# Five output stores issued in two column halves, so that the last store uses SyncE's last completion semaphore

**Chip and metric.** One core of one Trainium2 chip. The metric is the device time of one execution in microseconds (us), lower is better.

## The reference

A gated linear attention over 768 steps feeds a mixture of four dense experts; every expert is computed for every token.

```python
def _attn_ref(q, k, v, f_logit):            # (4, 8, 768, 48) each
    f = 1.0 / (1.0 + np.exp(-f_logit))
    for t in range(S):
        state = f[:, :, t, :, None] * state + einsum('bhd,bhe->bhde', k[:, :, t], v[:, :, t])
        y[:, :, t] = einsum('bhd,bhde->bhe', q[:, :, t], state)

def _moe_ref(x, domain_probs, w1, w2):      # x: (3072, 384); w1: (4, 384, 1024); w2: (4, 1024, 384)
    p = domain_probs / (domain_probs.sum(-1, keepdims=True) + 1e-09)
    for e in range(4):
        out += p[:, e:e + 1] * (np.maximum(x @ w1[e], 0.0) @ w2[e])
```

## The kernel before

The kernel works through six chunks of 128 time steps (`c`), each with four batches (`nt` or `b`). It keeps a list of steps, orders them with a small plan of its own and then issues them in that order. The output tile of (c, nt) is 128 x 384 in float32, 192 KB, and is stored by SyncE. Only the very last tile, (5,3), is already finished and stored in two column halves.

```python
    def store(c, nt, cols):
        r0 = nt * S + c * T
        nc.sync.dma_start(out=out[r0:r0 + T, cols], in_=tl("o", c, nt)[:, cols])
    ...
    def add_o(c, e, nt, half):
        by_cols = (c, e, nt) == (C - 1, E - 1, B - 1)
        part = half if by_cols else 0
        cols = slice(half * Din // 2, (half + 1) * Din // 2) if by_cols else slice(0, Din)
        ...
            if e == E - 1:
                P.add(f"store {c}.{nt}.{part}", {"DMA": 0.6}, lambda _: store(c, nt, cols), p - 25, deps=[ev], frees=[("o", c, nt)])
    ...
    with _tile.TileContext(nc) as tc:
        tile_hgrn2_outer__then__branch_train_merge_kernel(tc, *args)
```

Some words used below. SyncE is the engine that here issues transfers and waits for them. A semaphore is a counter by which one piece of work tells another that it is done; a wait is *satisfied* if its counter is already there when it is asked. A transfer has *landed* when it has reported that its last bytes are written. An *eviction* copies a result of the matmuls out of their accumulator memory. A *drain* is the instruction by which an engine lets its own work finish, and a *barrier* makes all engines wait for each other.

No line of the kernel says which semaphore a transfer reports to. The framework gives SyncE's transfers eight completion semaphores in turn, HW0 to HW7, and at the end of the program it makes SyncE wait for all of them in that order:

```
the end of SyncE's program, kernel before (one line is one instruction)
transfer: store (5,3), second half     -> reports to HW2
wait  DMASW7, DMASW6
wait  HW0, DMASW5
wait  HW1, DMASW4
wait  HW2, DMASW3        <- the last store
wait  HW3, DMASW2
wait  HW4, DMASW1
wait  HW5, DMASW0
wait  HW6, DVE
wait  HW7, Activation
drain (waits for Pool), first barrier of the engines, second barrier
```

## Time and profile before

| | kernel before |
|---|---|
| time, median of the first 3 runs | 298.62 us (298.36 to 298.94) |
| span of the profile | 296.6 us |
| TensorE busy | 97% |
| last eviction on VectorE ends | 293.68 us |
| last store issued, landed | 293.709, 295.348 us |
| SyncE's wait for it ends, its drain starts | 295.365, 295.733 us |

The last two rows come from the trace's own records of SyncE, which have nanoseconds; the views round to 0.1 us. "Landed" is the moment of the last of the 16 increments of the transfer's semaphore.

### The profile page before, as it was taken

Reading aid. Unit: us, or ns where it says so; the run is one execution under the profiler, and the core shown is the slowest. Engines: PE = TensorE matmul, PEld = TensorE weight load, DVE = VectorE, ACT = ScalarE, POOL = GpSimd, SP = SyncE. Lnnn points to the kernel's source line nnn. Section 1 sums busy time; section 2 is a strip of 40 time slices with the busy share of each in tenths; the row PEclk is TensorE's granted clock in tenths of the full one; section 3 lists DMA queues with packets and bytes.
Section 4 is the critical chain, followed back from the end, with each engine's and each line's share of the span. In section 5 each row is a group of like instructions: output and inputs, shape, how many; then the busy total and the mean of one; then the engine's idle time right before and its main releaser. Section 6 shows DMA issues by size and latency. Waiting matters only on the chain.

```text
span 296.6 us, 5591 instructions
## 1 busy us (share of the span) xinstructions
PE 289.0 (97%) x2172; PEld 170.0 (57%) x2172; DVE 126.1 (43%) x250; ACT 174.3 (59%) x317; POOL 106.1 (36%) x180
## 2 busy tenths in 40 slices
PE   6899999999999999999999999999999999999995
PEld 2476555567777775555555555555555555555553
DVE  6786012785763673045375235243523222101223
ACT  5656656666684667777477575554475544465440
POOL 5786401138767448144449372243220000000000
PEclk9999999999999999999999999999999999999999
DMA  7999999998979999998979932102432100200002
GB/s 157 200 169 206 207 192 210 189 210 167 201 152 166 191 171 185 209 187 164 198 133 218 179 60 35 27 0 67 122 61 30 27 2 27 80 2 0 0 2 106
DMA packets 136462, 36.43 MB, mean 123 GB/s; under 512 B 126812, under 2 KB 135644, under 8 KB 136436
## 3 DMA queue, kind: packets, MB, share of 16 engines
q1 hardware_dynamic: 125188, 29.35, 52.0%
q0 software_dynamic: 11248, 6.72, 16.4%
q8 instruction: 17, 0.28, 0.4%
q14 instruction: 9, 0.07, 0.1%
HBM read 31.51 MB, written 4.72 MB: 122 GB/s over the span
## 4 chain that ended last, share of the span: by engine, by line
PE 78%; DMA 14%; POOL 3%; SPq 2%; issue 1%; ACT 1%; DVE 0%; POOLq 0%
PE ps_m L389 37%; PE ps_m L374 35%; DMA w_sb<-in_moe_w_dram 10%; DMA k<-in_k_dram 4%; SPq L237 2%; POOL w_sb L246 2%; PE ps_t L325 2%; PE ps_t L340 1%; PE ps_t L336 1%; PE ps_t L273 1%; POOL vb L233 1%; PE ps_t L346 1%; ACT e L293 1%; DVE o L396 0%; ACT xT L226 0%
## 5 line engine op out<-in xcount | busy, mean ns | idle before, releaser
L385 ACT ACTIVATE h<-ps_m 128x512 bf16<-128x512 f32 (+2 forms) x188 | 102.4, 548 | 91.9 <-PE ps_m L374 88.9
L374 PE MATMUL ps_m<-xT,w_sb 128*128 128x512 bf16 (+3 forms) x708 | 152.8, 339 | 0.6 <-ACT xT L226 0.6
L389 PE MATMUL ps_m<-w_sb,h 128*128 128x384 bf16 (+1 forms) x776 | 152.6, 324 | 0.1
L389 PEld LDWEIGHTS <-h 128*128 128x128 bf16 x776 | 75.0, 98 | 59.0 <-DMA w_sb<-in_moe_w_dram 0.3
L396 DVE SCALAR_TENSOR_TENSOR o<-ps_m,pn,o 128x384 f32<-128x384 f32 (+1 forms) x73 | 44.5, 612 | 117.3 <-PE ps_m L389 111.1
L374 PEld LDWEIGHTS <-w_sb 128*128 128x128 bf16 x708 | 65.3, 98 | 43.5 <-issue 0.7
L301 POOL TENSOR_TENSOR qk<-q,e 128x384 bf16<-128x384 f32 x18 | 21.4, 1195 | 36.5 <-ACT e L293 34.3
L360 POOL TENSOR_TENSOR Sf<-Sf,egs 48x192 f32<-48x192 f32 x40 | 20.2, 504 | 36.5 <-DVE Sf L353 34.4
L329 DVE TENSOR_TENSOR AT<-ps_t,mask 128x512 bf16<-128x512 f32 x48 | 30.2, 683 | 5.1 <-PE ps_t L325 5.1
L383 DVE TENSOR_SCALAR h<-ps_m 128x256 bf16<-128x256 f32 (+2 forms) x40 | 19.3, 499 | 26.5 <-PE ps_m L374 13.1
L293 ACT ACTIVATE e<-ps_t 128x384 f32<-128x384 f32 x48 | 26.7, 668 | 5.0 <-PE ps_t L273 3.5
L301 POOL TENSOR_TENSOR qk<-k,e 128x384 bf16<-128x384 f32 x20 | 20.2, 1013 | 8.7 <-ACT e L293 5.5
L353 DVE TENSOR_TENSOR Sf<-Sf,ps_t 48x192 f32<-48x192 f32 x40 | 14.0, 350 | 10.3 <-PE ps_t L346 9.4
L246 POOL DMA_DIRECT2D w_sb<-in_moe_w_dram x11 | 8.8, 807 | 18.5 <-DMA k<-in_k_dram 17.2
L361 POOL CAST sb<-Sf 48x192 bf16<-48x192 f32 x40 | 13.6, 340 | 2.6
L398 ACT ACTIVATE o<-ps_m,pn 128x384 f32<-128x384 f32 x22 | 12.8, 582 | 2.5 <-PE ps_m L389 1.5
L644 PE MATMUL ps_m<-busy 128*128 128x512 bf16 x34 | 10.9, 423 | 1.5 <-DVE busy L144 1.5
L265 ACT ACTIVATE ex<-f 128x768 f32<-128x768 f32 (+1 forms) x14 | 10.4, 746 | 1.8 <-DMA f<-in_f_logit_dram 1.8
L298 POOL DMA_DIRECT2D egs<-e x16 | 9.0, 563 | 6.9 <-ACT e L293 6.9
L340 PE MATMUL ps_t<-vb,AT 128*128 128x48 bf16 x192 | 11.4, 184 | 0.0
L269 ACT ACTIVATE gp<-ex 128x768 bf16<-128x768 f32 (+1 forms) x14 | 10.5, 751 | 0.3
L340 PEld LDWEIGHTS <-AT 128*128 128x128 bf16 x192 | 9.9, 97 | 1.1
(54 smaller groups left out, 120.6 us busy)
## 6 DMA issues: line engine op xcount, KB each, us to landing
out_dram<-o SPq DMA_DIRECT2D x23, 192.0 KB, 2.0
w_sb<-in_moe_w_dram POOLq DMA_DIRECT2D x5, 768.0 KB, 18.0
k<-in_k_dram SPq DMA_DIRECT2D x10, 384.0 KB, 5.6
q<-in_q_dram SPq DMA_DIRECT2D x10, 384.0 KB, 5.5
v<-in_v_dram SPq DMA_DIRECT2D x10, 384.0 KB, 5.7
f<-in_f_logit_dram SPq DMA_DIRECT2D x9, 384.0 KB, 4.6
w_sb<-in_moe_w_dram POOLq DMA_DIRECT2D x6, 384.0 KB, 9.0
f<-in_f_logit_dram SPq DMA_DIRECT2D x6, 192.0 KB, 3.8
```

What stands on the lines that cost most here:

```text
L246: ins["w", i] = nc.gpsimd.dma_start(out=w[:, e, ks, cols], in_=r[e][:, ks, cols])
L293: nc.scalar.activation(out=o, in_=i, func=AF.Exp, scale=1.0 if j else -1.0)
L301: engines[eng].tensor_tensor(out=tl("qk", c, b)[:, j, :, 0:D].rearrange("t (i r) d -> t i r d", r=2), in0=tl("qk"[j], c, b // 2)[:, hh(b), ...
L329: nc.vector.tensor_tensor(out=tl("AT", c, b)[:, r].rearrange("s i t -> s (i t)"), in0=tl("A", c, b, r).rearrange("s i t -> s (i t)"), in1= ...
L340: nc.tensor.matmul(out=y[:, h * D:(h + 1) * D], lhsT=AT[:, r, i, :], rhs=vb[:, h, :], start=(c == 0), stop=True, skip_group_check=True)
L353: nc.vector.tensor_tensor(out=Sf[rows, b], in0=Sf[rows, b], in1=KV[rows, :, r, :], op=ALU.add)
L360: nc.gpsimd.tensor_tensor(out=Sf[rows, b], in0=Sf[rows, b], in1=eg, op=ALU.mult)
L374: nc.tensor.matmul(out=hp(c, e, fc, n0, n1, nf)[:, f], lhsT=w1_sb[:, e, kk, (fc + f) * 128:(fc + f + 1) * 128], rhs=tl("xT", c)[:, kk, n0: ...
L383: nc.vector.tensor_relu(out=dst, in_=src)
L385: nc.scalar.activation(out=dst, in_=src, func=AF.Relu)
L389: nc.tensor.matmul(out=tl("op", c, e, nt, part)[:, cols], lhsT=tl("h", c, e, half_of(c, nt * T))[:, fc, nt * T:(nt + 1) * T], rhs=w2_sb[:, ...
L396: nc.vector.scalar_tensor_tensor(out=o, in0=op, scalar=pe, in1=o, op0=ALU.mult, op1=ALU.add)
```

## The change

The intent is to move the last store from HW2 to HW7, so that no wait for an already complete semaphore stands between its landing and the end. Five more transfers in front of it do that, since the semaphores go in turn. They are got by cutting five earlier stores in two.

```diff
+    halved = [(C - 3, B - 1)] + [(C - 2, nt) for nt in range(B)]
+
     def store(c, nt, cols):
         r0 = nt * S + c * T
-        nc.sync.dma_start(out=out[r0:r0 + T, cols], in_=tl("o", c, nt)[:, cols])
+        parts = [slice(i * Din // 2, (i + 1) * Din // 2) for i in range(2)] if (c, nt) in halved else [cols]
+        for p in parts:
+            nc.sync.dma_start(out=out[r0:r0 + T, p], in_=tl("o", c, nt)[:, p])
```

## The prediction

> **What bounds the kernel now.** I read the head of the page first, then the chain of work that ended last, then the last microseconds of that chain, and only then SyncE (SP), which the page hardly mentions because all of it is sequencer work and none of it counts as busy.
>
> ```profile
> span 296.6 us, 5591 instructions
> PE 289.0 (97%) x2172; PEld 170.0 (57%) x2172; DVE 126.1 (43%) x250; ACT 174.3 (59%) x317; POOL 106.1 (36%) x180
> ...
> PE 78%; DMA 14%; POOL 3%; SPq 2%; issue 1%; ACT 1%; DVE 0%; POOLq 0%
> ```
>
> TensorE is busy for 97% of the span and is 78% of the chain. The chain for 286 to 297 us shows how it ends: 44 output matmuls of line 389, then one 0.42 us eviction on VectorE that ends at 293.68 us. Columns are start, length, what.
>
> ```profile
> 287.35 5.88 PE ps_m L389 x44
> 293.24 0.03 issue
> 293.26 0.42 DVE o L396
> ```
>
> From 293.68 to 296.6 no compute runs: these 2.9 us are the last store and the end of the program. The chain view stops short of them, so I asked SyncE's own waits from 293.9 us on (total us, times, longest), and which instructions the two lines concerned issue there (durations in ns, first and last start in us).
>
> ```profile
> SPq L674 <- DMA out_dram<-o: 1.1, 3, 0.6
> SPq L674 <- PEq L674: 0.7, 2, 0.5
> ```
>
> ```profile
> L404 SPq DMA_DIRECT2D out_dram<-o x5: 332/333/350, 290.0 to 293.7; - x5
> ...
> DMA to landing us min/median/max: 1.6/1.8/1.9
> ```
>
> ```profile
> L674 SPq EVENT_SEMAPHORE x6: 28/28/28, 295.4 to 295.7; - x6
> ```
>
> The last line is asked for the window 295.3 to 295.72 us alone. The last store is issued at 293.71 us and lands 1.64 us later, at 295.348. Then SyncE runs six wait instructions. The first is the one that waits for this store. The other five wait for semaphores that are long complete, and still take up 295.4 to 295.7. The trace's records, finer than the view's tenths, have their starts at 295.365, 295.427, 295.486, 295.547, 295.607 and 295.668, and the drain that follows at 295.733. So one satisfied wait costs 0.0606 us from start to start (0.303 us over five), of which the profile reports 0.028 as execution.
>
> Why five are left is in the built program: at the end SyncE waits, in this fixed order, for the DMA completion semaphores HW0, HW1, ... HW7 (each wait shared with one other semaphore), after one wait for two of GpSimd's DMA semaphores. DMAs of SyncE take HW0 to HW7 in turn. In the kernel before the last store is on HW2, so HW3 to HW7 are asked after it.
>
> **What the Trainium skill says.** "Perfetto Trace Analysis", section "Sequencer-only Instruction (DRAIN, etc)": the profiler reports execution alone, and neither the wait before it nor the readiness for the next instruction. The trace agrees: 28 ns is reported of a 60 ns step, so the step and not the duration is the cost. "Advanced Engine Details and Errata", section "Network/Comms": reading a semaphore's value from a sequencer takes 50 to 100 ns on trn2. The 60 ns step here lies in it, although each instruction names two semaphores. "DMA: Bandwidth & Descriptors", section "Anatomy of one DMA — SWDGE (gpsimd) path": most of a DMA's fixed cost of about 2 us is the receipt that its last byte has landed. Here the last 96 KB store, on the hardware path, needed 1.64 us to land and the 192 KB stores about 1.9: halving the bytes saves little, and nothing in the change shortens the last store.
>
> **The change part by part.** Five stores of 192 KB, tiles (3,3) and (4,0) to (4,3), become two of 96 KB each. The order of the built programs shows what else moves.
>
> Added on SyncE: five DMA issues. One issue is 0.33 us, with its semaphore wait and the gap some 0.38 (the store at 213.012 is followed by the next transfer at 213.447, 0.435 later, including a two-semaphore wait). The sum is 5 x 0.38 = 1.9 us of SyncE time. Beside what does it lie? SyncE's timeline around the first one:
>
> ```profile
> 207.66 5.68 SPq L404 DMA_DIRECT2D out_dram<-o  x3
> 213.45 1.24 SPq L314 DMA_TRANSPOSE QK<-qk  x1
> 216.59 4.32 SPq L318 DMA_TRANSPOSE xT<-yb  x2
> ```
>
> The second half of (3,3) pushes the transpose at 213.45 to about 213.83. It then ends its issue at 215.07 instead of 214.69. The next transfer, at 216.59, waits for its input, so 1.5 us of slack take up the 0.38 and nothing later moves. The delayed transpose lands at about 216.9 instead of 216.5, and its matmuls (line 325) run at 226.8. The four stores of (4,x) are issued at 249.8, 252.4, 255.0 and 257.5, 2.6 us apart, with nothing behind them until 289.99. On the path: 0.
>
> Added on the DMA rings: no bytes. 128 packets of 1,536 bytes become 256 of 768 per store, 640 more of 136,462, in stretches where the DMA share is 0.36 (200 to 215 us) and 0.06 (250 to 288 us). On the path: 0.
>
> Added waits elsewhere: three wait instructions on ScalarE and three on VectorE, because a reused output buffer now waits for two halves. The kernel's two reused buffers of tiles (4,0) and (4,1) are first written at 264.7 and 267.3, against second halves landing at about 252 and 254.5: 12 us of slack, so none blocks. On ScalarE the wait is taken while the 0.60 us eviction before it runs. VectorE idles there for 2 us at a time for TensorE. On TensorE the count of instructions and their order are the same, with other semaphore numbers. On the path: 0.
>
> Moved: ten halves where there were five stores shift all later SyncE DMAs by five places in the turn, so the last store goes from HW2 to HW7. A DMA also waits for the one eight places earlier on its semaphore. With the halves these eight places span less time, but the closest pair I find is about 15 us apart in issue (the transpose of 221.00 behind that of 206.28, which landed at 209.34), and the final five stores wait for stores of 250 to 258 us. No new wait.
>
> At the end: HW0 to HW4 are waited for before 294.4, HW5 (store landed 294.411) and HW6 (294.691) pass as HW0 and HW1 did, HW7 passes at 295.365, and the drain follows one step later at 295.43 instead of 295.733. What comes after, the two barriers between the engines, starts when SyncE arrives last (VectorE, the next to last, arrived at 293.745), and keeps its length: 296.6 - 295.73 = 0.87 us. The sum is -5 x 0.0606 = -0.303 us: a span of 296.3, and 298.62 - 0.30 = **298.32 us** timed, if the 2.0 us by which the timed run exceeds the span stay.
>
> **The rivals.** First, the waits are cheaper than they look: tracing itself may lengthen each sequencer step, or the drain may have to wait for something else. For it: I have the step from a profiled run only. Against: SyncE is the last to reach the barrier by 2 us, and the records show nothing else between the sixth wait and the drain. The result would be 298.4 to 298.6. Second, the extra issues delay a transpose that TensorE needs. For it: the SyncE queue is in order and the transpose at 213.45 is directly behind the first split store. Against: the slack of 1.5 us on the queue and 9.9 us at the consumer, and TensorE without a gap from 200 to 250 us. If a wait were created it could cost at most one issue per split on the path, 298.7 to 300. Third, a split store frees its buffer later, or a semaphore's earlier user is not done, and an eviction waits. Against: the 12 us above. It would cost a few tenths. Fourth, the gain is real and lost in the scatter: three runs before range over 0.58 us, twice the gain. This does not move the median expected, but does widen the range.
>
> **Range and chances.** The centre is 298.32. The first rival moves it up by at most 0.3, the scatter of a median by some 0.3 either way, and the others upward by some tenths with little chance. So 297.95 to 298.75 should hold it 8 times in 10. Two per cent are 6.0 us, twenty times the gain and more than all that follows the last matmul (3.4 us): faster by that is as good as excluded, and slower would need a stall that no slack above leaves room for.
>
> **What would show it right or wrong.** Right: line 678, as it is then numbered, has one satisfied wait after the last landing in place of six, its total on SyncE after the last landing falls by 0.3, the span is about 296.3, the last matmul still ends near 293.24, the transpose of 213.45 starts about 0.38 later and that of 216.59 does not move. Wrong: the last eviction ends later than 293.7 (a stall in the middle), the last store takes longer than 1.7 us to land, or the wait for HW7 is followed by another of 0.3 us.

## The result

| | before | changed |
|---|---|---|
| median of 6 runs of the same rounds | 298.78 us (297.85 to 299.49) | 298.88 us (297.94 to 299.76) |
| span of the profile | 296.6 us | 296.0 us |
| last eviction on VectorE ends | 293.682 | 293.474 |
| last store, issue to landing | 1.639 | 1.613 |
| wait for it ends to drain starts | 0.368 | 0.065 |
| landing to the end of the span | 1.232 | 0.928 |

The ratio of the times is 1.0005, with a 95% interval of 0.9987 to 1.0024: the same. Here and below a ratio is the one for two kernels measured together; it is not quite the ratio of the medians.

The two measures seem to contradict each other: the profile is 0.54 us shorter, the timed runs are not. But a profile is of one run: that of the changed kernel took 297.94 us, the fastest of its six. The profile can be taken apart. First the end of SyncE. Asked for the instructions of the end (now line 678) between 295.1 and 295.27 us, the changed kernel shows one wait and then the drains:

```profile
L678 SPq DRAIN  x2: 7/10/13, 295.2 to 295.3; - x2
L678 SPq EVENT_SEMAPHORE  x1: 28/28/28, 295.1 to 295.1; - x1
```

The kernel before has six waits there, from 295.4 to 295.7. SyncE's own waits from 293.3 us on (total us, times, longest) say the same from the other side: only two waits for stores are left where there were three, and the barrier costs what it did.

```profile
SPq L678 <- DMA out_dram<-o: 0.8, 2, 0.6
SPq L678 <- PEq L678: 0.7, 2, 0.5
```

The extra half of store (3,3) shows on SyncE's timeline of the changed kernel as four stores where there were three. The transpose behind it starts at 213.72, and the next one, at 216.38, is where it was but for the 0.2 us by which this whole profile is ahead:

```profile
207.45 6.16 SPq L408 DMA_DIRECT2D out_dram<-o  x4
213.72 1.24 SPq L314 DMA_TRANSPOSE QK<-qk  x1
216.38 4.32 SPq L318 DMA_TRANSPOSE xT<-yb  x2
```

These 0.2 us are the other part. The chain of the changed kernel for 286 to 297 us:

```profile
287.15 5.88 PE ps_m L389 x44
293.03 0.02 issue
293.06 0.42 DVE o L396
```

The last 44 matmuls take the same 5.88 us, but begin at 287.15 instead of 287.35. To see where that came from I set the two traces side by side, weight load by weight load (all 2,172 are in every trace). The offset wavers up to the 437th, near 59 us. From there to the last one, 234 us later, it stays between -0.213 and -0.206. The chains between 57 and 61 us tell what was different there. Before:

```profile
50.37 8.82 DMA w_sb<-in_moe_w_dram
59.19 0.05 issue
59.24 1.47 PE ps_m L389 x8
```

and changed:

```profile
58.32 0.45 PE ps_t L310 x8
58.76 0.33 PE ps_t L325 x8
59.09 1.41 PE ps_m L389 x8
```

In the kernel before, TensorE waited until a load of expert weights landed at 59.19; in the profile of the changed kernel those weights were there in time (none of TensorE's waits up to 62 us names a load). The change touches nothing before 200 us, so this counts as luck; the kernel before, profiled twice, differs from itself by as much there (0.19 us, next section). The profile's 0.537 us are then 0.207 of luck ahead of 59 us, 0.303 of waits, and 0.027 of the last landing.

This makes two claims to test. **My theory:** the move is worth 0.30 us in every execution and the halves cost nothing, but loads in the first 60 us make each run scatter by more than that. **Rival A:** the halves cost in the middle what the end gains. **Rival B:** the waits do not set the end. **Rival C:** the scatter is not in the head, but everywhere.

### The profile page after: what moved, and what is told of

It is laid out like the page before. It is cut to its first block, busy times and chain, and to the rows that moved or that the text cites. A ratio compares the mean times of both kernels' runs of the same rounds, so it can differ in the third digit from the quotient of the medians.

```text
span 296.0 us, 5574 instructions
## 1 busy us (share of the span) xinstructions
PE 287.7 (97%) x2144; PEld 170.2 (58%) x2172; DVE 126.1 (43%) x250; ACT 174.3 (59%) x317; POOL 106.1 (36%) x180
## 4 chain that ended last, share of the span: by engine, by line
PE 93%; SPq 2%; DMA 2%; issue 1%; ACT 1%; DVE 0%
PE ps_m L389 42%; PE ps_m L374 42%; SPq L237 2%; PE ps_t L325 2%; DMA q<-in_q_dram 2%; PE ps_t L340 2%; PE ps_t L336 1%; PE ps_t L346 1%; PE ps_t L273 1%; PE ps_t L310 1%; PE ps_m L648 1%; ACT e L293 1%; PE ps_t L365 0%; ACT QK L226 0%; PE ps_m L256 0%
## 5 line engine op out<-in xcount | busy, mean ns | idle before, releaser
L374 PE MATMUL ps_m<-xT,w_sb 128*128 128x512 bf16 (+3 forms) x682 | 150.4, 338 | 1.7 <-ACT xT L226 0.6
```

The lines of the kernel that those rows point to most:

```text
L374: nc.tensor.matmul(out=hp(c, e, fc, n0, n1, nf)[:, f], lhsT=w1_sb[:, e, kk, (fc + f) * 128:(fc + f + 1) * 128], rhs=tl("xT", c)[:, kk, n0: ...
```

## The experiments

Twelve kernels ran on two chips. This table has what the records of all whole-kernel traces show, in us. "Head" is the start of the 437th weight load, "middle" the time from it to the last weight load. "Waits" counts the satisfied waits after the last landing.

| kernel | last store on | waits | head | middle | wait ends to drain | landing to end |
|---|---|---|---|---|---|---|
| before | HW2 | 5 | 59.233 | 233.664 | 0.368 | 1.232 |
| before_again | HW2 | 5 | 59.419 | 233.668 | 0.368 | 1.232 |
| changed | HW7 | 0 | 59.020 | 233.670 | 0.065 | 0.928 |
| after_again | HW7 | 0 | 59.207 | 233.666 | 0.065 | 0.912 |
| halve8 | HW2 | 5 | 59.358 | 233.670 | 0.368 | 1.219 |
| first6 | HW0 | 7 | 59.282 | 233.671 | 0.494 | 1.336 |
| early5 | HW7 | 0 | 59.743 | 233.666 | 0.065 | 0.929 |
| halve16 | HW2 | 5 | 59.833 | 233.666 | 0.707 | 1.680 |
| halve21 | HW7 | 0 | 59.736 | 233.664 | 0.068 | 0.933 |
| hidden14 | HW2 | 5 | 59.740 | 233.671 | 0.759 | 1.827 |
| hidden6 | HW2 | 5 | 59.545 | 233.664 | 0.368 | 1.312 |
| late6 | HW2 | 5 | 59.906 | 233.666 | 0.368 | 1.746 |
| waits48 | HW2 | 5 | 61.286 | 233.668 | 0.368 | 4.641 |

### Both kernels again

No edit: the kernel before, timed against itself, and the changed kernel.

> The kernel before, unchanged, timed against itself. Theory (the waits after the last landing are worth 0.30 us, and the arrival of the first loads scatters each run by more): the ratio lies within 0.2% of 1 with single times some 1.5 us apart; in the profile, the drain of SyncE starts 0.37 us after the last wait that a landing released (five satisfied waits of 0.0606 us), whatever the span; and the span's difference from the other profile of this kernel is there in full by 60 us. Rival (the scatter sits in the middle or at the end): the offset between the two profiles still grows after 60 us.

> The changed kernel once more. Theory: 0.065 us from the last wait released by a landing to the drain, so 0.30 us less at the end than the kernel before in the same call, and a ratio of 0.997 to 1.001, too wide to see 0.1%. Rival A (the halved stores cost somewhere in the middle what the end gains): the distance from the output matmuls near 60 us to the last one is longer than in the kernel before by about 0.3 us. Theory: that distance is the same within 0.02 us.

Measured: 298.97 us median (298.34 to 300.78) for the kernel before against 298.71 (297.95 to 299.85) for itself, ratio 1.0016 (0.9987 to 1.0045); 298.38 (298.09 to 298.67) for the changed kernel, ratio 0.9987 (0.9968 to 1.0007). A kernel against itself came out further from 1 than either comparison with the change. In the profiles all went as my theory expects: 0.368 and 0.065 us again, the middles alike to 2 ns, and the whole difference between the two profiles of the kernel before, 0.19 us, present at the 437th weight load (+0.186) and unchanged at the last (+0.190).

### The halves without the move

```diff
-    halved = [(C - 3, B - 1)] + [(C - 2, nt) for nt in range(B)]
+    halved = [(C - 3, nt) for nt in range(B)] + [(C - 2, nt) for nt in range(B)]
```

> Eight stores halved instead of five, so that the last store comes back to the third completion semaphore: the halves alone, without the move. Theory: five satisfied waits after the last landing as in the kernel before, 0.37 us to the drain, no difference from it in the middle (within 0.02 us), ratio 1.000 within scatter. Rival A: eight extra issues of 0.38 us show as 0.3 us or more between 60 us and the last matmul.

Measured: 298.65 us, ratio 0.9999 (0.9976 to 1.0021). With eight halves the middle is 233.670 us, as before, and the tail is that of the kernel before. Asked for 295.49 to 295.9 us, the end shows its six waits again:

```profile
L678 SPq EVENT_SEMAPHORE  x6: 27/28/28, 295.5 to 295.8; - x6
```

So inside the span halves alone neither cost nor gain. Rival A falls for these places.

### The worst semaphore

```diff
-    halved = [(C - 3, B - 1)] + [(C - 2, nt) for nt in range(B)]
+    halved = [(C - 3, nt) for nt in range(2, B)] + [(C - 2, nt) for nt in range(B)]
```

> Six stores halved, so that the last store lands on the first of the eight semaphores, the worst place. Theory: seven satisfied waits follow the last landing, 0.065 + 7 x 0.0606 = 0.49 us from the released wait to the drain, 0.12 more than before and 0.42 more than the changed kernel, nothing in the middle. Rival B (the waits overlap, or something else than SyncE sets the end): the distance from the last landing to the end stays that of the kernel before, 1.25 us, instead of 1.35.

Measured: 299.08 us, ratio 1.0014 (0.9988 to 1.0039). In the profile, for 295.38 to 295.95 us:

```profile
L678 SPq EVENT_SEMAPHORE  x8: 28/28/28, 295.4 to 295.8; - x8
```

The one that waited, and seven more; 0.494 us to the drain, 0.49 expected. With 0, 5 and 7 waits the time to the drain is 0.065, 0.368 and 0.494, a straight line of 0.061 a wait, and the end of the span follows it to 0.02 us (0.928, 1.232 and 1.336 from landing to end). Rival B falls.

### Other places for the halves

```diff
-    halved = [(C - 3, B - 1)] + [(C - 2, nt) for nt in range(B)]
+    halved = [(0, nt) for nt in range(B)] + [(1, 0)]
```

> Five other stores halved, the first five of the run, where SyncE's queue and the DMA engines are busy; the last store lands on the last semaphore all the same. Theory: 0.065 us from the released wait to the drain as in the changed kernel; the middle (59 us to the last matmul) may be longer where a load or a transpose is pushed by 0.38 us, and if it is not, the place of the halves does not matter. Rival A (halves cost 0.3 us or more where the queue is busy): the middle is 0.3 us or more above 233.67 us.

Measured: 298.78 us, ratio 1.0011 (0.9981 to 1.0041). Middle 233.666, wait to drain 0.065. For the middle the place does not matter even in the busy first half.

### Many more waits

The edit is to the kernel before. The compiler joins two waits into one instruction, so 96 make 48.

```diff
     with _tile.TileContext(nc) as tc:
         tile_hgrn2_outer__then__branch_train_merge_kernel(tc, *args)
+    done = nc.alloc_semaphore(name="done")
+    nc.sync.sem_inc(done, 1)
+    for _ in range(2 * 48):
+        nc.sync.wait_ge(done, 1)
+    nc.sync.sem_clear(done)
```

> The kernel before, with 48 more satisfied waits of two semaphores on SyncE after its end, then one clear of the semaphore. Theory: each step is 0.0606 us, so the span is 48 x 0.0606 = 2.91 us longer, some 3.1 with the increment and the clear, and the timed run with it: about 301.8 us, ratio 1.010. Rival B (a wait's price is only in the profile's spacing, or a run of waits overlaps): less than 1.5 us more, ratio under 1.005.

Measured: 302.51 us, ratio 1.0121 (1.0093 to 1.0150), 3.6 us more; landing to end is 3.41 us longer in the profile. The waits are real time in the timed runs, whose interval allows 2.8 to 4.5 us. In the profile the excess over the expected 3.1 is one gap: after ten waits SyncE stood still for 0.35 us (halve16 takes this up), while the last 36 steps are 0.0606 us each.

This profile also caught a late head. In the chain for 57 to 61 us there is only a load of weights, which lands at 61.25 us; the kernel before had it at 59.19:

```profile
51.79 9.46 DMA w_sb<-in_moe_w_dram
```

The waits of the weight loads on TensorE up to 62 us (total us, times, longest), of which the kernel before has only the first line, with 0.3 us in it:

```profile
PEld L389 <- DMA w_sb<-in_moe_w_dram: 1.4, 2, 1.2
...
PEld L374 <- DMA w_sb<-in_moe_w_dram: 0.8, 2, 0.6
```

The span of 302.0 us is, against the kernel before, 2.05 us of late head, most of it waits for weights, and 3.41 us of the waits added; the middle is 233.668 us, as in all the others. The weights were late because of something earlier: in the chain of this profile the first load of `k` lands at 12.88 us, in that of the kernel before at 11.05, and the loads of weights follow it.

### Waits ahead of the landing

14 waits in the kernel before, placed behind the issue of the last store and so ahead of its landing (the semaphore is allocated ahead of the context and cleared after it):

```diff
         o.emit(o.engine)
+    nc.sync.sem_inc(tc.done, 1)
+    for _ in range(2 * 14):
+        nc.sync.wait_ge(tc.done, 1)
```

> The kernel before with 14 satisfied waits and one increment on SyncE directly behind the issue of the last store, so ahead of its landing. Theory: 15 x 0.0606 = 0.91 us of them, with the three waits that the end has there 1.09, begin 0.38 us after the issue and so end at about 1.5 us, before the landing at 1.64: landing to end stays 1.23 us and the time that of the kernel before (one clear at the very end may add 0.1 to 0.2). Rival (every wait costs where it stands): 0.9 us more, ratio 1.003.

Measured: 299.11 us, ratio 1.0009 (0.9985 to 1.0033). The profile missed what I expected: landing to end is 1.827 us, 0.6 more than before. Two things went wrong in my edit. The branch to the program's end took 0.18 us with the new wait on it, so the wait for the last store was reached 0.07 us after the landing. And SyncE again stood still, for 0.36 us, this time between the last wait and the drain. The next two runs mend this with six waits, once ahead of the landing and once after the end.

```diff
+    for _ in range(2 * 6):          # hidden6: ahead of the landing, where the 14 were
+    for _ in range(2 * 6):          # late6: after the end, where the 48 were
```

> The run with 14 waits again with 6, so that they end well ahead of the landing and SyncE's program stays short of its 207th instruction, at which two profiles showed a gap of 0.35 to 0.36 us. Theory: the increment and six waits, some 0.44 us, with the slower branch behind them (0.18) and three waits of the end (0.18) end 1.2 us after the last store's issue, ahead of the landing at 1.62: from the landing to the start of the last semaphore wait of the second barrier it is 1.17 us, as in the kernel before; only the clear at the very end adds 0.07 to 0.1. Rival (a satisfied wait costs wherever it stands): 0.4 us more.

> The same six waits and the increment, but after the end. Theory: 0.5 us more in the span than in the kernel before from the landing to the end (0.08 for the increment, 6 x 0.061, one clear), against 0.1 in the run with the same six ahead of the landing. Rival: the same in both.

Measured: hidden6 298.60 us, ratio 0.9992 (0.9966 to 1.0018); late6 299.63, ratio 1.0025 (1.0000 to 1.0050). Landing to end is 1.312 us with the six waits ahead of the landing, 0.080 more than the kernel before, which is the clear of the semaphore; up to the last wait of the second barrier it is 1.166 against 1.169. With the same six waits after the end it is 1.746, 0.514 more. The place decides. The lines for hidden6 show its six waits done before 295 us and the landing's six untouched (the second fence is for 295.65 to 296.05 us):

```profile
L648 SPq EVENT_SEMAPHORE  x6: 17/28/28, 294.5 to 294.8; - x6
```

```profile
L678 SPq EVENT_SEMAPHORE  x6: 27/28/28, 295.7 to 296.0; - x6
```

### Does the head alone scatter?

Cut off after the steps that the plan starts before 120 us. Its output is wrong, which doesn't matter for the time.

```diff
-    for o in done:
+    for o in [o for o in done if o.start < 120.0]:
```

> Wrong on purpose: the kernel before cut off after the steps that its own plan starts before 120 us, so that most of the output is not written. Theory (the scatter of the timed runs is made by the arrival of loads in the first 60 us): about 125 us, and the runs spread over as many microseconds as those of the whole kernel, 1 us or more between the lowest and the highest. Rival C (the scatter is made over the whole length, by the clock or otherwise): a spread in proportion to the length, under 0.7 us where the whole kernel has 1.9.

Measured: 121.7 us, four runs from 121.34 to 122.09, a spread of 0.75 us; 11 runs of the kernel before spread over 2.28. Four runs are too few: my theory asked for 1 us or more, the rival for under 0.7, and the result lies between. This run does not decide. Its profile sides with the theory: against the first profile of the kernel before it is 0.461 us late at the 437th weight load and 0.463 late at the last weight load that both have, at 116 us.

### Where the gap of 0.35 us comes from

In both earlier cases the gap came just ahead of the same SyncE record of the trace, number 207 counted from zero. The kernel before has 196 records, so it ends short of it. Sixteen halves put it between the last wait and the drain, with the last store on HW2 again; twenty-one put it ahead of the last landing, with the store on HW7.

```diff
-    halved = [(C - 3, B - 1)] + [(C - 2, nt) for nt in range(B)]
+    halved = [(c, nt) for c in range(C) for nt in range(B)][4:20]     # halve16
+    halved = [(c, nt) for c in range(C) for nt in range(B)][0:21]     # halve21
```

> Sixteen stores halved: the last store is on the third semaphore as in the kernel before, but the sixteen more instructions of SyncE put its 207th recorded instruction between the landing and the first barrier. If the gap of 0.35 us belongs to that place in SyncE's program, it shows there: landing to end 1.23 + 0.36 = 1.59 us. If it belonged to the added waits of the two earlier runs, landing to end stays 1.23. The middle stays at 233.67 if halves cost nothing.

> Twenty-one stores halved, all but the last three: the last store lands on the last semaphore as in the changed kernel, and the 207th instruction falls among the waits ahead of the last landing. Theory: 0.065 us from the released wait to the drain, landing to end 0.92 us, the gap of 0.35 us hidden ahead of the landing, middle 233.67. Rival A (halves cost): 21 x 0.38 us of issue show in the middle or in the last stores, 0.3 us or more.

Measured: halve16 299.27 us, ratio 1.0012 (0.9989 to 1.0036); halve21 298.27, ratio 0.9987 (0.9960 to 1.0015). In halve16 the gap is where it was put. Asked for 295.95 to 296.8 us:

```profile
L678 SPq EVENT_SEMAPHORE  x6: 28/28/28, 296.0 to 296.3; - x6
L678 SPq DRAIN  x1: 130/130/130, 296.7 to 296.7; - x1
```

The last wait ends at 296.33 and the drain starts at 296.67, 0.35 us later, and itself takes 130 ns instead of 13. Landing to end is 1.680 us, 0.09 more than my 1.59, which the slower steps on either side of the gap make up. In halve21 the same gap (0.37 us, ahead of record 207) falls before the landing and costs nothing: 0.933 us from landing to end. Both middles are 233.66 to 233.67, so even 16 and 21 halves cost nothing there.

The pages of these runs show something that goes with the gap. Within the span, the queue that the page calls "instruction" moved 9 packets in the kernel before and in eight more of the 13 profiles of whole kernels. In the four with the gap (waits48, hidden14, halve16, halve21) it moved 10:

```profile
q14 instruction: 9, 0.07, 0.1%
```

```profile
q14 instruction: 10, 0.08, 0.1%
```

In the trace's records the tenth packet, of 8 KB, starts 0.61 to 0.65 us after SyncE goes on, each time. So SyncE's stop comes with a fetch of more instructions. That the fetch is what it stops for is not shown.

## Why the prediction was right or wrong

**Right: the step's price and what the move saves inside the span.** 0.0606 us a wait, five of them, -0.303 us predicted. Measured in the profiles: 0.368 - 0.065 = 0.303. Runs with 0, 5, 7 and, outside the end, 36 waits in a row give the same step.

**Right: the halves cost nothing inside the span.** The transpose behind the first half was predicted 0.38 us later; freed of the profile's offset of 0.207 it came 0.48 later (213.72 + 0.21 - 213.45), because an issue that carries its own semaphore wait took 0.423 us in place of 0.333. The slack took it up as said. The middle is the same within 7 ns in 13 profiles, with 0, 5, 6, 8, 16 or 21 halves.

**Right: satisfied waits are not cheaper than they look, in these runs.** The added waits lengthened the timed runs by 3.6 us (2.8 to 4.5) where the profile has 3.4. Whether a step costs the same with no tracing at all stays open: every run has a span on record, so every run was traced.

**Wrong: what the timed run has beyond the span does not stay.** The prediction carried the gain from the span to the time "if the 2.0 us by which the timed run exceeds the span stay". The 2.0 took a median of three runs and the span of one. The record has time and span of the same run, with the span to 0.1 us, for 30 runs of the kernel before and for all 12 of the changed kernel:

| kernel | runs | time less span, mean (lowest to highest) |
|---|---|---|
| before | 30 | 1.72 us (1.66 to 1.78) |
| changed | 12 | 1.88 us (1.83 to 1.94) |

The two do not overlap. (With waits added behind the end it is less: late6 has 1.40, waits48 1.27.) So some 0.16 of the 0.30 us came back outside the span, and what the timed runs could gain was about 0.14. Other kernels show that it is neither the halves nor the last semaphore as such: early5 has 1.86 us, first6 1.96, halve8 1.80, but halve16 1.72 and halve21, whose last store is on HW7 too, 1.73. Where no waits were added, the higher values belong to the four kernels whose SyncE program has 201 to 204 records, ending a little short of the record 207 where the gap stands; the kernel before has 196, and halve16 and halve21 have the gap inside the span. A gap that falls behind the last record would fit. It is not shown: the trace of halve8 has another instruction packet 1.6 us after its span, but that of the changed kernel has none. The cause stays open.

**Wrong: the scatter and the base.** The measured 298.88 us lies outside the stated 297.95 to 298.75. The other step that failed is the one that gave "the scatter of a median by some 0.3 either way", together with the base of 298.62 as if it were exact. Both rest on three runs that happened to lie within 0.58 us. Thirty-six runs of the same kernel lie between 297.78 and 300.78, with a standard deviation of 0.71 and a median of 298.79. From that deviation, the median of six runs has a standard error of some 0.36 us (an estimate: 1.25 x 0.71 / 2.45), so a range for 8 in 10 had to be about 0.46 either side for this term alone. Of the 0.56 us by which the result lies above the centre of 298.32, 0.17 is then the base (298.79 in place of 298.62), 0.16 the part outside the span, and the remaining 0.23 is within that standard error. All 12 runs of the changed kernel have a median of 298.46 and a mean of 298.59, against a mean of 298.85 for the 36: 0.25 us less, with a standard error of 0.18. That fits -0.14 as well as -0.30 and does not exclude zero. The gain inside the span is shown by the profiles; no gain is shown by the timed runs.

**Where the scatter is made.** In 13 profiles of whole kernels the head varies by 2.27 us (59.02 to 61.29), the middle by 0.007, and the tail is set by the waits. The page of the kernel before named a candidate, 14% of the chain on transfers, mostly of expert weights, and I read past it because the change does not touch it. Loads explain the late head of waits48 and the 0.21 us between the first two profiles. They do not explain every head: in early5 and halve16, 0.5 and 0.6 us later than the kernel before, none of TensorE's waits up to 62 us names a load, and what made them late is not shown. That every slow timed run was slow in its head is inferred from the profiles: of the other runs only span and clock are on record, and the clock of the slowest, 300.78 us, is 1.0 like that of the fast ones.

## What to carry to other kernels

What stands behind the last landing is on the path instruction by instruction, even where every wait is satisfied; the same instructions ahead of the landing cost nothing. So count what the end of a program still does after its last transfer, and let that transfer be the one that is waited for last. And before a gain of 0.1% is forecast, take the scatter from more than three runs, and look for the stage that makes it: a change of this size is proved by a stretch of the trace that does not scatter. Then compare time less span as well: what the span gains can be lost outside it.

## What the Trainium skill lacked or had wrong

- **The price of a satisfied wait at the end of a program.** "Advanced Engine Details and Errata", section "Network/Comms", gives 50 to 100 ns for reading a semaphore from a sequencer. The step here is 0.0606 us, in that range, and the same whether the instruction's two semaphores are different or one and the same. No page says that the waits at the end stand in a fixed order behind the last transfer, where each one is paid in full: 0.30 us for five.
- **A gap in SyncE's program.** "Runtime: NRT & Kernel Launch", section "Instruction fetch mechanics", has instructions fetched in blocks of 256, and calls the cost of crossing one "mostly hidden". Four profiles (waits48, hidden14, halve16, halve21) show SyncE standing still for 0.35 to 0.37 us ahead of its record 207, with slower steps around it; behind the last landing it cost 0.45 us (halve16). The place follows the count of SyncE's instructions, and each time one more packet of instructions (10 in place of 9) follows 0.61 to 0.65 us after SyncE goes on. So such a crossing is likely, and not hidden here; that it is the cause is not shown, as the trace does not record all that SyncE executes.
- **The scatter of one kernel on one core.** No page has it: 36 runs of the unchanged kernel lie over 3.0 us (1.0%) at a granted clock of 0.998 to 1.0 (30 of them have it on record), and the profiles put the differences into the first 60 us.
